# Attention products of the first stage gathered into fewer groups on TensorE, with the last two batches and the hand-over laid out anew

## The chip, the cores and the metric

One of the eight cores of a Trainium2 chip runs the whole program; the seven others are idle. The metric is the device time of one execution in microseconds (us), the median of several runs. A core has TensorE (PE in the profile, with its weight loads as PEld), VectorE (DVE), ScalarE (ACT), GpSimd (POOL) and SyncE (SP, which here issues the DMAs). Each engine works through its own instructions in order, and waits at an instruction for what that instruction needs.

## The reference

Attention with packed queries over eight batches of 576 tokens and eight heads, then two feed-forward layers on all 4,608 tokens.

```python
def sm_attn(qq, kk, vv):
    s = scale * np.matmul(qq, kk.transpose(0, 1, 3, 2))
    s = s - np.max(s, axis=-1, keepdims=True)
    a = np.exp(s)
    a = a / (np.sum(a, axis=-1, keepdims=True) + 1e-09)
    return np.matmul(a, vv)
p_packed = sm_attn(p, k, v)            # 32 packed rows a head
out = sm_attn(q, p_packed, p_packed)   # (8, 8, 576, 64)
...
h = x @ w_in                           # (4608, 512) @ (512, 2048)
x = (h * np.cos(h)) @ w_out            # back to 512
h = x @ w_in2
g = np.where(h >= 1, h, np.where(h <= -1, 0.0, (h + 1) ** 2 / 4))
y = g @ w_out2
```

## The kernel before

The program runs in four stages: the first holds the attention and the first layer up to h; then come h * cos(h) with w_out, w_in2, and w_out2. Only the first stage and its end are touched. All is float32: the large products split each operand into a high and a low part of type fp32r and add three of the four partial products (`TERMS`).

**The first stage** is a list of 128 items, 16 to a batch n. An item (`up`, line 513) is 12 products of 288 columns: it multiplies the second attention's weights `at` of half a batch by a matrix `M` and leaves 256 rows of h for 288 tokens in the PSUM tile `hps` (tag "h", two buffers). ACT copies `hps` into a buffer `u` of SBUF (line 519; four buffers), and SP stores `u` to DRAM as `h1T`; a buffer is free when its store has landed. `M` is the packed values times w_in, one chunk c of 512 columns for four items, in two buffers.

**What else TensorE does in the first stage**, for the batches that come next (`m = n+1` and `m = n+2`), is put between the items by a list of slots: whatever is listed at slot i is issued just ahead of item i. These products are small, and I call them by letters:

- K: `scores1`, packed queries by keys, for half of the 576 tokens (8 products of 288 columns, tile psS).
- T: `turn1`, the transposes of the first attention's weights for one of the two head halves (5 transposes); ACT copies them out as `e` (lines 265 and 266).
- V: `values1`, the weights `e` by the values, for two of the four head pairs (20 products of 32 columns, line 276); ACT copies the sum out as `pt` (line 283).
- Q: `scores2`, queries by packed keys, for half of the tokens (8 products of 288 columns); DVE transposes them out of PSUM (line 294, two instructions a half).
- F: `form`, packed values by w_in for one chunk of `M` (8 products of 512 columns, tile psM); ACT copies the high part out (line 341), DVE the low part (line 343).

K, Q and F use a quarter-by-half tile of the array each, eight at a time. The trace counts every plain float32 product twice. psS and psM are one PSUM tile each, of two banks: whoever writes one waits until it has been read out. `S1` and `S2` are the slots, within a batch, of the steps of the first attention of batch n+2 and of the second of batch n+1; the tuple in the call of `formed` holds those of F. K, T and V, and both halves of Q, go to psS; F goes to psM.

**DVE and ACT** also turn w_out and w_in2 into split form in this stage: `cut_w_out` is a generator of small steps (16 rows f; lines 138 to 157, 391 and 397), of which `WO_SHARE` lets some run behind certain items, and 1.2 us worth behind each item of the last batch. Its loads use two buffers `raw`, so row f+2 is asked for once row f is done.

**The end of the stage.** `begin` issues, ahead of the last six items, the first steps of h * cos(h): `turn_k` to `part_lo` (lines 694 to 721), that make r, the operand of the next stage. That stage sums in PSUM tiles X and Y for even blocks and two tiles Z for odd ones. They take over the banks of "h" and of psS and psM in the order in which they are first asked for: X and Y fall on the two "h" tiles.

A list written in Python sets the order on every engine; no scheduler changes it.

## Time and profile before

| | |
|---|---|
| median of 3 runs | 1497.51 us (1496.89 to 1499.18) |
| the profiled execution, its own time | 1489.83 us |
| its span, first to last instruction | 1488.1 us |
| TensorE busy | 1459.3 us, 98% |
| VectorE, ScalarE busy | 1164.9 us, 908.3 us |
| mean granted clock of TensorE | 0.996 |
| first stage, from the first item to the first product of the next stage | 34.7 to 356.5 us |

TensorE is the busy engine, and from 357 us on it is never idle for long. In the first stage it is busy too, but not all the time, and some of its busy time is spent in changing between small and large products. In a timeline each row gives start, duration, engine, line, operation, out<-in, shape and count of a run of equal instructions, then in brackets how long the engine stood idle before it and what it waited for. Durations of such runs overlap a little at the ends, so the cost of a group is read from its start to the start of the next. A row of waits gives the engine, who waits, for whom, the sum, the number of times and the longest.

### The profile page before, as it was taken

How to read it: one execution, taken by the hardware profiler on the slowest of the kernel's cores; microseconds unless marked ns; L12 is line 12 of the kernel's file. 1: busy time of each engine (PE TensorE's matmuls, PEld its weight loads, DVE VectorE, ACT ScalarE, POOL GpSimd, SP SyncE). 2: the span in 40 equal slices, each digit the busy share in tenths (PEclk: the TensorE clock that was granted, in tenths of full speed). 3: DMA queues.
4: the chain of work that ended last, by engine and by line, in shares of the span. 5: the costliest groups of instructions: out<-in, count | busy, mean ns of one | idle time of the engine just before them, and what ended most of it. 6: DMA issues, size and time to landing. Idle time of an engine off the chain costs nothing.

```text
span 1488.1 us, 29660 instructions
## 1 busy us (share of the span) xinstructions
PE 1459.3 (98%) x11796; PEld 1394.7 (94%) x11796; DVE 1164.9 (78%) x1683; ACT 908.3 (61%) x1424; POOL 134.0 (9%) x85
## 2 busy tenths in 40 slices
PE   8899999998999999999999999999999999999998
PEld 5678777888999999999999999999999999999998
DVE  8885677777898888888856888889868777777875
ACT  4555565657666667666656777877765444444443
POOL 0000000000000000000004435434310000000000
PEclk9999999999999999999999999999999999999999
DMA  9776787477555665866573555654578654344350
GB/s 351 244 245 245 240 285 263 176 264 236 179 159 162 200 186 184 275 217 199 170 273 130 205 181 213 219 180 181 212 290 331 237 160 142 108 130 140 120 160 33
DMA packets 156058, 302.36 MB, mean 203 GB/s; under 512 B 13584, under 2 KB 59664, under 8 KB 152336
## 3 DMA queue, kind: packets, MB, share of 16 engines
q1 hardware_dynamic: 155920, 300.47, 59.7%
q8 instruction: 92, 1.51, 0.4%
q14 instruction: 46, 0.38, 0.1%
HBM read 176.69 MB, written 123.73 MB: 202 GB/s over the span
## 4 chain that ended last, share of the span: by engine, by line
PE 86%; DVE 5%; DMA 5%; ACT 2%; issue 1%; SPq 0%; ACTq 0%; DVEq 0%
PE psZ L748 14%; PE hps L513 10%; PE psZ L955 10%; PE psZ L610 9%; PE psX L748 7%; PE psY L748 7%; PE psX L955 7%; PE psY L955 6%; PE psX L610 6%; PE psY L610 6%; DMA h1T<-u 3%; PE psS L276 1%; PE psM L219 1%; DMA t<-gT 1%; PE psS L219 1%
## 5 line engine op out<-in xcount | busy, mean ns | idle before, releaser
L513 PEld LDWEIGHTS hps<-at,m 128*128 128x128 f32 x1536 | 209.6, 190 | 48.4 <-ACT u L519 18.6
L513 PE MATMUL hps<-at,m 128*128 128x288 f32 x1536 | 227.4, 303 | 10.1 <-ACT at L329 4.7
L748 PE MATMUL psZ<-r,wo 128*128 128x288 f32 x1536 | 206.1, 295 | 0.0
L748 PEld LDWEIGHTS psZ<-r,wo 128*128 128x128 f32 x1536 | 205.2, 188 | 0.0
L858 ACT ACTIVATE r<-g 128x576 fp32r<-128x576 f32 x147 | 97.0, 681 | 122.8 <-DVE g L855 113.7
L77 POOL TENSOR_TENSOR ty<-yb,ty 128x576 fp32r<-128x576 f32 x51 | 86.2, 1691 | 950.3 <-ACT ty L76 949.8
L716 ACT ACTIVATE r<-t 128x576 fp32r<-128x576 f32 x128 | 87.7, 685 | 129.1 <-PE psY L748 62.1
L721 DVE TENSOR_TENSOR r<-t,r 128x576 fp32r<-128x576 f32 x128 | 96.9, 757 | 57.8 <-ACT r L716 57.6
L519 ACT ACTIVATE u<-hps 128x576 f32<-128x576 f32 x128 | 83.1, 650 | 93.7 <-PE hps L513 57.9
L748 PE MATMUL psX<-r,wo 128*128 128x288 f32 x768 | 123.3, 296 | 1.7 <-ACT u L519 1.7
L748 PE MATMUL psY<-r,wo 128*128 128x288 f32 x768 | 123.2, 296 | 0.0
L630 DVE SCALAR_TENSOR_TENSOR t<-hh,t 128x576 f32<-128x576 f32 x128 | 121.8, 971 | 0.0
L622 ACT ACTIVATE t<-hh,half 128x576 f32<-128x576 f32 x128 | 98.9, 772 | 33.2 <-DVE hh L598 31.2
L868 DVE TENSOR_TENSOR r<-g,r 128x576 fp32r<-128x576 f32 x147 | 107.3, 751 | 5.2 <-ACT r L858 5.2
L748 PEld LDWEIGHTS psX<-r,wo 128*128 128x128 f32 x768 | 109.4, 188 | 2.0 <-ACT u L519 2.0
L748 PEld LDWEIGHTS psY<-r,wo 128*128 128x128 f32 x768 | 109.4, 188 | 0.0
L955 PE MATMUL psZ<-r,so 128*128 128x288 f32 x768 | 104.8, 295 | 0.6 <-DVE hh L991 0.6
L955 PE MATMUL psY<-r,sw 128*128 128x288 f32 x768 | 104.6, 295 | 0.0
L955 PEld LDWEIGHTS psZ<-r,so 128*128 128x128 f32 x768 | 102.9, 188 | 0.8 <-DVE hh L991 0.8
L955 PEld LDWEIGHTS psY<-r,sw 128*128 128x128 f32 x768 | 102.8, 188 | 0.0
L711 DVE TENSOR_TENSOR t<-h,t 128x576 f32<-128x576 f32 x128 | 96.1, 751 | 2.2 <-ACT t L706 2.2
L706 ACT ACTIVATE t<-t,halfpi 128x576 f32<-128x576 f32 x128 | 97.6, 762 | 0.0
(163 smaller groups left out, 2642.2 us busy)
## 6 DMA issues: line engine op xcount, KB each, us to landing
h1T<-u SPq DMA_DIRECT2D x128, 288.0 KB, 3.9
h<-h1T SPq DMA_DIRECT2D x128, 288.0 KB, 3.8
gT<-t SPq DMA_DIRECT2D x128, 288.0 KB, 3.2
g<-gT SPq DMA_DIRECT2D x85, 288.0 KB, 3.6
raw<-in_moe_w_out SPq DMA_DIRECT2D x32, 512.0 KB, 6.9
raw<-in_moe_w_in SPq DMA_DIRECT2D x28, 512.0 KB, 6.4
t<-gT SPq DMA_DIRECT2D x36, 288.0 KB, 4.4
k<-in_k SPq DMA_DIRECT2D x8, 1152.0 KB, 9.0
```

The source lines that it names most:

```text
L513: nc.tensor.matmul(out=hps[:, j, :HB], lhsT=m[:, w, G, cs], rhs=x[:, G, y], start=(G == 0 and i == 0), stop=(G == 1 and i == 2),)
L610: nc.tensor.matmul(out=ps[:, i], lhsT=s[:, d, w, cs], rhs=t[:, d, y], start=first and d == n == 0, stop=d == 1 and n == 2, skip_group_chec ...
L622: nc.scalar.activation(out=t, in_=st["h", o], func=AF.Relu, scale=0.5, bias=half)
L630: nc.vector.scalar_tensor_tensor(out=t, in0=st["h", o], scalar=1.0, in1=t, op0=ALU.max, op1=ALU.min)
L706: nc.scalar.activation(out=t, in_=t, func=AF.Sin, scale=2 * PI, bias=halfpi)
L711: nc.vector.tensor_tensor(out=t, in0=G1.pop(i), in1=t, op=ALU.mult)
L716: nc.scalar.activation(out=r[:, 0], in_=turns[i], func=AF.Copy)
L721: nc.vector.tensor_tensor(out=r[:, 1], in0=turns.pop(i), in1=r[:, 0].bitcast(F32), op=ALU.subtract)
L748: nc.tensor.matmul(out=acc[d // 2][:, d % 2], lhsT=wo[f // 4, w][:, f % 4, ds], rhs=r[:, y, k], start=f == n == 0, stop=f == NFT - 1 and n ...
L858: nc.scalar.activation(out=r[:, 0], in_=b[out], func=AF.Copy)
L868: nc.vector.tensor_tensor(out=r[:, 1], in0=src, in1=r[:, 0].bitcast(F32), op=ALU.subtract)
L955: nc.tensor.matmul(out=ps[:, j], lhsT=w_[:, (2 * c + k) % 4, w, j * 128:j * 128 + 128], rhs=r[:, y, k], start=first_k and k == n == 0, sto ...
```

## The change

The slots move so that small products stand together and fewer runs of items lie between them. V becomes one group for all four head pairs, ordered by chunks of 128 tokens, with the heads inside a chunk; only the first chunk's first product clears the sum. The second half of T and the second half of Q go to psM. There are five buffers `u`. F of chunks 1 and 2 stands one item earlier, F of chunk 0 one item later (behind Q), and in the last two batches the low part of the last chunk is cut an item earlier. `WO_LAST` and `WO_MORE` spread the steps of w_out over the last two batches. `begin` starts one item earlier. The two Z tiles of block 1 are asked for first, so they take the banks of "h", and X and Y those of psS and psM.

```diff
+WO_LAST = (1.2, 0, 0, 1.2, 0, 0, 1.2, 1.2, 0, 0, 1.2, 0.6, 0.6, 0.7, 0, 0.7)
+WO_MORE = {3: 0.7, 7: 0.7, 10: 0.7, 11: 0.7}
...
-    def values1(m, G, tag="psS"):
-        if G == 0:
-            PV[m] = double(tag)
-        for hp in (2 * G, 2 * G + 1):
-            for i, (_, n) in enumerate(chunks):
+    def values1(m, tag="psS"):
+        PV[m] = double(tag)
+        for i, (_, n) in enumerate(chunks):
+            for hp in range(HP):
                 for h2 in range(2):
...
-                        rhs=E32[m][:n, h2, i, J * hp:J * hp + J], start=(i == 0), stop=(i == KC),
+                        rhs=E32[m][:n, h2, i, J * hp:J * hp + J], start=(i == hp == 0), stop=(i == KC),
+                        skip_group_check=True,
...
-        u = wk.tile([128, 2, HB], F32, tag="u", name="u", bufs=4)
+        u = wk.tile([128, 2, HB], F32, tag="u", name="u", bufs=5)
...
-                acc = [bank("Z") for _ in range(2)] if blk % 2 else [bank(x) for x in "XY"]
+                acc = early if blk == 1 else [bank("Z") for _ in range(2)] if blk % 2 else [bank(x) for x in "XY"]
...
-        a, b, c, d = scores1(m, 0), scores1(m, 1), turn1(m, 0), turn1(m, 1)
+        a, b, c, d = scores1(m, 0), scores1(m, 1), turn1(m, 0), turn1(m, 1, "psM")
...
-        a, b, c, d, e = scores2(m, 0), scores2(m, 1), soft2(m, 0, 4, V), turn2(m, 0, V), turn2(m, 1, V)
+        a, b, c = scores2(m, 0), scores2(m, 1, "psM"), soft2(m, 0, 4, V)
...
-    S1 = (3, 3, 4, 4, 5, 7, 9, 11, 11, 12, 12, 13, 14, 15)
-    S2 = (1, 1, 2, 2, 3, 4, 5, 7, 8, 9, 10, 10, 11, 12, 13)
+    S1 = (2, 3, 4, 4, 5, 7, 9, 11, 11, 11, 11, 13, 14)
+    S2 = (1, 1, 1, 1, 3, 4, 5, 7, 8, 9, 10, 10, 11, 12, 13)
...
-                formed(j, shifted(base + 4 * c, (1, 1, 2)))
+                formed(j, shifted(base + 4 * c, ((2, 2, 3), (0, 0, 1), (0, 0, 1), (1, 1, 1 if n > B - 3 else 2))[c]))
...
-            if i >= len(items) - 6:
-                for x in begin[i - len(items) + 6]:
+            if i >= len(items) - 7:
+                for x in begin[i - len(items) + 7]:
...
-                t, share = 0.0, 1.2 if i >= 16 * (B - 1) else WO_SHARE.get(i % 16, 0)
+                t, share = 0.0, WO_LAST[i % 16] if i >= 16 * (B - 1) else WO_SHARE.get(i % 16, 0) or (i > 96 and WO_MORE.get(i % 16, 0))
...
+    early = [bank("Z"), bank("Z")]
```

The first place is TensorE early in batch n = 3 (pt_121 are the packed values of batch 4, x12 is one item). Before:

```order
L219 MATMUL psS<-q,pt_121 32x288 x8
L219 MATMUL psM<-wi,pt_124 32x512 x8
L513 MATMUL hps<-at,m 128x288 x12
L219 MATMUL psS<-q,pt_121 32x288 x8
L513 MATMUL hps<-at,m 128x288 x12
L219 MATMUL psS<-k,pp 32x288 x8
L513 MATMUL hps<-at,m 128x288 x12
L219 MATMUL psS<-k,pp 32x288 x8
L513 MATMUL hps<-at,m 128x288 x12
L219 MATMUL psM<-wi,pt_124 32x512 x8
L513 MATMUL hps<-at,m 128x288 x48
```

The same place on TensorE now:

```order
L219 MATMUL psS<-q,pt_121 32x288 x8
L219 MATMUL psM<-q,pt_121 32x288 x8
L513 MATMUL hps<-at,m 128x288 x12
L219 MATMUL psS<-k,pp 32x288 x8
L219 MATMUL psM<-wi,pt_124 32x512 x8
L513 MATMUL hps<-at,m 128x288 x24
L219 MATMUL psS<-k,pp 32x288 x8
L219 MATMUL psM<-wi,pt_124 32x512 x8
L513 MATMUL hps<-at,m 128x288 x48
```

Both Q stand together, in two tiles, and each K stands with an F; the runs of items in front of the long one are two in place of four, and one item lies between the Q in psM and the K and F that need psS and psM again.

The second place is ACT late in the same batch, where it empties T (e) between the copies u of the items and the copy at of the second attention's weights. Before:

```order
L519 ACTIVATE u<-hps 128x576
L265 ACTIVATE e_1757<-psS 128x512
L266 ACTIVATE e_1757<-psS 64x128
L519 ACTIVATE u<-hps 128x576
L329 ACTIVATE at<-a_1755 128x2x288
L265 ACTIVATE e_1757<-psS 128x512
L266 ACTIVATE e_1757<-psS 64x128
L519 ACTIVATE u<-hps 128x576
```

The same place on ACT now:

```order
L519 ACTIVATE u<-hps 128x576
L265 ACTIVATE e_1757<-psS 128x512
L266 ACTIVATE e_1757<-psS 64x128
L265 ACTIVATE e_1757<-psM 128x512
L266 ACTIVATE e_1757<-psM 64x128
L519 ACTIVATE u<-hps 128x576
L329 ACTIVATE at<-a_1755 128x2x288
L519 ACTIVATE u<-hps 128x576
```

The second half of e no longer stands behind a u and an at.

The third place is DVE at the start of batch n = 6, where it empties Q (x<-psS) behind the steps of w_out. Before:

```order
L151 TENSOR_SCALAR raw<-w_3387 128x512
L153 SCALAR_TENSOR_TENSOR raw<-raw 128x512
L397 TENSOR_TENSOR wo<-w_3318,wo 128x512
L294 STREAM_TRANSPOSE x<-psS 128x288 x4
L343 TENSOR_TENSOR m<-psM,m 128x1024
L301 TENSOR_REDUCE mx_3481<-x 128x36
```

The same place on DVE now:

```order
L151 TENSOR_SCALAR raw<-w_3387 128x512
L153 SCALAR_TENSOR_TENSOR raw<-raw 128x512
L397 TENSOR_TENSOR wo<-w_3338,wo 128x512
L294 STREAM_TRANSPOSE x<-psS 128x288 x2
L294 STREAM_TRANSPOSE x<-psM 128x288 x2
L301 TENSOR_REDUCE mx_3480<-x 128x36
L343 TENSOR_TENSOR m<-psM,m 128x1024
```

What stands ahead of the transposes is the same; F's low part (line 343) has moved behind them and behind the first reduction.

## Rows read from the trace of the kernel before

**Rows 1.** The page's first line.
```profile
span 1488.1 us, 29660 instructions
```

**Rows 2.** Timeline of TensorE early in batch 1.
```profile
90.62 0.72 PE L219 MATMUL psS<-kv,pt 64*32 64x288 f32 x16
91.13 1.06 PE L219 MATMUL psM<-wi,pt 64*32 64x512 f32 x16
92.12 1.87 PE L513 MATMUL hps<-at,m 128*128 128x288 f32 x12
93.93 0.71 PE L219 MATMUL psS<-kv,pt 64*32 64x288 f32 x16
94.57 1.86 PE L513 MATMUL hps<-at,m 128*128 128x288 f32 x12
...
102.27 6.66 PE L513 MATMUL hps<-at,m 128*128 128x288 f32 x48
108.86 1.09 PE L219 MATMUL psM<-wi,pt 64*32 64x512 f32 x16
```

**Rows 3.** Timeline of TensorE before the first item: two Q together, then F.
```profile
24.60 1.21 PE L219 MATMUL h<-kv,pt 64*32 64x288 f32 x32 [0.38 <-ACT pt L283]
25.59 1.07 PE L219 MATMUL psM<-wi,pt 64*32 64x512 f32 x16
```

**Rows 4.** Waits of TensorE from 90 to 290 us (batches 1 to 5), all of them.
```profile
PE psS L261 <- ACT e L266: 2.1, 2, 1.8
PE psS L276 <- ACT e L266: 1.9, 2, 1.3
PE psS L219 <- DVE x L294: 1.3, 2, 1.0
PE hps L513 <- ACT u L519: 1.0, 3, 0.5
```

**Rows 5.** Timelines late in batch 2: ACT, then TensorE.
```profile
155.54 0.65 ACT L519 ACTIVATE u<-hps 128x576 f32<-128x576 f32 x1 [2.27 <-DMA h1T<-u]
157.45 1.72 PE L276 MATMUL psS<-e,v 128*64 128x32 f32 x40 [1.28 <-ACT e L266]
```

**Rows 6.** Stretches: length, busy PE, PEld, DVE, ACT, POOL (instructions), granted clock, DMA share, GB/s.
```profile
34.70:90.60 55.90, 49.20 (x512) 39.56 (x512) 48.24 (x85) 31.49 (x57) 0.00 (x0) 0.94 0.74 242
44.60:52.30 7.70, 6.74 (x122) 4.51 (x122) 5.74 (x9) 4.85 (x10) 0.00 (x0) 1.00 0.68 213
158.50:163.50 5.00, 5.00 (x50) 3.10 (x46) 4.90 (x7) 1.03 (x1) 0.00 (x0) 0.66 0.18 62
```

**Rows 7.** Timelines of TensorE and DVE where batches 3, 4 and 6 begin with Q.
```profile
170.11 0.72 PE L219 MATMUL psS<-q,pt 64*32 64x288 f32 x16
173.51 0.84 DVE L294 STREAM_TRANSPOSE x<-psS 128x288 f32<-128x288 f32 x2
...
210.32 0.72 PE L219 MATMUL psS<-q,pt 64*32 64x288 f32 x16
212.98 0.84 DVE L294 STREAM_TRANSPOSE x<-psS 128x288 f32<-128x288 f32 x2
...
289.98 0.71 PE L219 MATMUL psS<-q,pt 64*32 64x288 f32 x16
293.45 0.84 DVE L294 STREAM_TRANSPOSE x<-psS 128x288 f32<-128x288 f32 x2
```

**Rows 8.** Timelines of ACT and TensorE in the last batch and at the hand-over.
```profile
334.88 0.65 ACT L138 ACTIVATE raw<-raw 128x512 f32<-128x512 f32 x1 [3.52 <-DMA raw<-in_moe_w_out]
...
337.04 2.14 PE L513 MATMUL hps<-at,m 128*128 128x288 f32 x14 [2.01 <-ACT u L519]
...
356.50 1.07 PE L748 MATMUL psX<-r,wo 128*128 128x288 f32 x6 [1.72 <-ACT u L519]
```

**Rows 9.** Timeline of TensorE in batch 0, the first T between items.
```profile
76.39 0.76 PE L261 MATMUL psS<-ident,s 128*128 128x128 f32 x5 [0.78 <-DVE s L254]
```

More of the change, by code (lines that the diff above doesn't have):

```diff
@@ L18 @@
 WARM = (10, 14, 10)
-PRI_EXP = 300
 WO_FROM = 36
@@ L27 @@
 WO_SHARE = {0: 1.2, 6: 0.7, 12: 1.3, 13: 1.3, 14: 1.3, 15: 1.3}
-PRI_MAIN = 300
+WO_LAST = (1.2, 0, 0, 1.2, 0, 0, 1.2, 1.2, 0, 0, 1.2, 0.6, 0.6, 0.7, 0, 0.7)
+WO_MORE = {3: 0.7, 7: 0.7, 10: 0.7, 11: 0.7}
 FIRST = ((0, 0), (0, 1), (1, 0), (1, 1), (0, 2), (1, 2), (0, 3), (1, 3))
@@ L1037, in first @@
     def first(m, o):
-        a, b, c, d = scores1(m, 0), scores1(m, 1), turn1(m, 0), turn1(m, 1)
+        a, b, c, d = scores1(m, 0), scores1(m, 1), turn1(m, 0), turn1(m, 1, "psM")
         steps = (nxt(a), nxt(a), nxt(b), nxt(b), lambda: max1(m), lambda: exp1(m), lambda: norm1(m),
-                 nxt(c), nxt(c), nxt(d), nxt(d), lambda: values1(m, 0), lambda: values1(m, 1), lambda: packed(m))
+                 nxt(c), nxt(d), nxt(c), nxt(d), lambda: values1(m), lambda: packed(m))
         for i, (s, x) in enumerate(zip(o, steps)):
@@ L1044, in first @@
                 on(s, lambda: load_k(m + 1))
-            if i == 13 and m + 1 < B:
+            if i == 12 and m + 1 < B:
                 on(s, lambda: load_v(m + 1))
     def second(m, o):
-        a, b, c, d, e = scores2(m, 0), scores2(m, 1), soft2(m, 0, 4, V), turn2(m, 0, V), turn2(m, 1, V)
-        for i, (s, g) in enumerate(zip(o, (a, a, b, b, c, c, c, c, c, d, d, d, e, e, e))):
+        a, b, c = scores2(m, 0), scores2(m, 1, "psM"), soft2(m, 0, 4, V)
+        d, e = turn2(m, 0, V), turn2(m, 1, V)
+        for i, (s, g) in enumerate(zip(o, (a, b, a, b, c, c, c, c, c, d, d, d, e, e, e))):
             on(s, nxt(g))
@@ L1074, in body @@
         if n == 0:
-            first(2, (6, 6, 7, 7, 9, 10, 11, 12, 12, 13, 13, 14, 15, 16))
+            first(2, (6, 6, 7, 7, 9, 10, 11, 12, 12, 12, 12, 14, 15))
         elif n + 2 < B:
@@ L1120, in start @@
         next(a), next(b)
-        values1(0, 0, "h")
-        values1(0, 1)
+        values1(0, "h")
         cut(5)
@@ L1159, in start @@
         cut(5)
-        values1(1, 0)
         next(m1)
-        values1(1, 1)
+        values1(1)
         load_v(2)
@@ L1188, in body @@
              [lambda: turn_s(1), lambda: turn_m(1), lambda: turn_k(3)],
-             [lambda: part_hi(0), lambda: part_lo(0), lambda: turn_s(2), lambda: part_hi(1)]]
+             [lambda: part_hi(0), lambda: part_lo(0), lambda: turn_s(2), lambda: part_hi(1)], []]
     in_order = ordered(E.PE, E.Activation, E.DVE, E.SP, E.Pool)
```

## The prediction

> **What bounds the kernel now.** I read the page first, then the stretches of the first stage, then TensorE's waits there, then its timeline row by row. The span is 1488.1 us [rows 1], and TensorE is the busy engine of all stages. The change touches only the first stage and the hand-over to the second, so the question is what TensorE spends there beyond its products, and which of its waits end on the work that is moved. Three things are to be seen. First, a run of items costs more than its items: one item takes from 92.12 to 93.93, 1.81 us, and four take from 102.27 to 108.86, 6.59 us [rows 2]. So a further item costs (6.59 - 1.81) / 3 = 1.593 us, and each run pays 1.81 - 1.593 = 0.217 us once, for passing to the small products. Second, in batches 1 to 5 TensorE waits 6.3 us in all, 4.0 of them for `e` (T's and V's waits), 1.3 for the transposes of Q, 1.0 for `u` [rows 4]. Third, the last stretch, from Q of batch 6 to the first product of the next stage, takes 356.50 - 289.98 = 66.5 us [rows 7, 8], and it holds waits of its own, 2.01 and 1.72 us being the largest [rows 8]. In the first batch it is DVE that is busy, 48.24 of 55.90 us [rows 6].
>
> **The change part by part.**
>
> **Grouping in batches 1 to 5.** Written in order, a batch on TensorE was QF 1 Q 1 K 1 K 1 F 4 F 2 T 1 T 1 VF 1 V 3 (digits are items), ten runs of items; it becomes QQ 1 KF 2 KF 4 F 3 TT 2 VVF 4, six runs. Four runs fewer save 4 x 0.217; but one of the four lies beside T, which uses the array in the same shape as the items, and I take half for it: 0.76 us. The small groups: Q ahead of F takes 90.62 to 91.13, 0.51; the F behind it 0.99; Q alone 0.64 [rows 2]. K is as large as Q. Before: QF 1.50, Q and two K 1.92, two F 1.98, together 5.40 us (VF and V aside). Two Q together took 0.99 us with F behind them [rows 3], and ahead of an item 0.13 more (0.64 against 0.51): 1.12. After: 1.12, twice KF 3.00, F 0.99, together 5.11. That is 0.29 less. Sum 1.05 a batch, and 5 batches give **5.2 us**. This is work of TensorE itself, so nothing hides it; it is worth less only where a wait takes its place.
>
> **V by chunks of tokens.** The number of products and of weight loads stays, and the two halves of the array alternate as they did. I take 0. The bounds are 0.1 us either way a group, by the 0.13 that a Q differs with its neighbour [rows 2]: 1 us over all batches, both ways. The last chunk's `e` is now needed last, which can only help.
>
> **T's second half in psM, the order of e on ACT, and five buffers u.** In batch 2 ACT stood 2.27 us at a `u` whose buffer was still being stored; the second `e` was queued behind that `u`, and V waited 1.28 us for it [rows 5]. Now the four `e` stand together ahead of that `u`, T's second half needs not wait for psS, two items lie between T and V, and a `u` waits for the store five items back, one item (1.6 us) more. So the 4.0 us for `e` go, and half of the 1.0 for `u` [rows 4]. Behind that wait the clock fell: granted 0.66 from 158.5 to 163.5 [rows 6], so 5.0 x 0.34 = 1.7 us were lost there; I count 1.6 as gone with it. Together 4.0 + 0.5 + 1.6 = 6.1 us.
>
> **Q's second half in psM.** Here a wait is added. DVE reaches the transposes of Q late, because steps of w_out stand ahead of them: 3.40 us behind the start of Q in batch 3, 2.66 in batch 4, 3.47 in batch 6 [rows 7], and what stands ahead of them does not change. A pair takes 0.84, so psS is free at 4.3 and psM at 5.2 us after the start of Q in batch 3 (0.1 for the signal). TensorE comes back to psS with K at 1.12 + 1.81 = 2.9, and to psM with F 0.51 later. K waits 1.4, F then 0.4: 1.8 us. In batch 4: psS 3.6, psM 4.4; waits of 0.6 and 0.3. Batch 5 I take as batch 4; in batches 1 and 2 no steps of w_out stand there yet, and I take none. Sum 1.8 + 0.9 + 0.9 = 3.6 us, in place of 1.3 [rows 4]: **2.3 us lost**. Between 1.3 (DVE is early) and 5 times 1.8 I keep 3.6, from the rows of these very batches. Queued behind the waiting K and F are two items, whose `u` come later by as much; DVE's softmax follows the transposes directly and starts earlier than before, so nothing else is late for it. The Trainium skill has a rule that speaks against this part (TensorEngine Tiling (Array Packing), PSUM Bottleneck): using the array in tiles speeds up the products, not their evacuation, which may become the bound. The rows agree so far as four transposes of 0.42 us stand against 1.12 us of Q; by the rule alone every batch would wait, which is the last rival below.
>
> Batches 1 to 5: 5.2 + 6.1 - 2.3 = **9.0 us**.
>
> **Batches 6 and 7 and the hand-over.** The new order is QQ 1 F 2 F 4 F 5 F 5 F 2 F 4 F 8, 31 items: 31 x 1.593 + 8 x 0.217 = 51.1; QQ 1.12; seven F 6.9: 59.2 us. Added waits: F behind the one item needs psM, free at 3.47 + 1.68 + 0.1 = 5.2, and comes at 2.9: 2.3 us. Of the steps of w_out, one row's load is asked for two items ahead of its use, as all were before; there ACT stood 3.52 us, and TensorE 2.01 [rows 8]. Now one such place is left, and I take half of 2.01: 1.0 us (between 0 and 2.0). Behind the last F, ACT has the copies of eight items, the last two rows of w_out and the first steps of the next stage; I estimate that it is late for the last items by 0.8 us (0 to 2.0, the wait that it caused before). X and Y lie on banks that were read out long before, so the wait of 1.72 us at the hand-over [rows 8] goes, and r is asked for one item earlier, so it isn't late in its place. Sum 59.2 + 2.3 + 1.0 + 0.8 = 63.3 against 66.5: **3.2 us**. What was moved to batch 6 (four shares of w_out, which has no first attention to do) lies on DVE and ACT beside items of TensorE; I cost it at nothing.
>
> **Batch 0.** DVE sets the pace up to the first T, which waited 0.78 us for it [rows 9]; a low part of `M` moves from ahead of one to ahead of another step of the same DVE chain, and I take half of that wait as gone, 0.4. Behind it two runs fewer save 0.4. Together **0.8 us** (0 to 2.5).
>
> **The sum** is 9.0 + 3.2 + 0.8 = 13.0 us off the profiled execution, whose span of 1488.1 becomes 1475.1 and whose own time of 1489.83 becomes 1476.8. The median of the runs lies 7.7 us above that execution; I take the same difference off it: 1497.5 - 13.0 = **1484.5 us**.
>
> **The rivals.**
>
> *The clock falls in the longer stretches of small products.* VVF is now 4.4 us without an item (two V of 1.72 [rows 5], F 0.99 [rows 2]). For it: the clock did fall while V and F ran, 158.5 to 163.5. Against it: from 44.6 to 52.3 there was no item for 7.7 us, only T, V, F and Q with gaps, and the granted clock stayed at 1.00, the 2.4 GHz level [rows 6]. Price: 1.7 us in each of five batches, 8.5: 1493.0. The Trainium skill (TensorE: Matmul & The Clock Gate, Part 1) says that the throttled clock is the default and that recent activity of the array releases it; by that rule fewer gaps help and longer thin stretches may not. Chance 0.08.
>
> *The waits for e and u stay.* If ACT is late for another reason, such as the loads of k that take the queue from the stores, the 6.1 us do not come: 1490.6. For it: a wait of 2.27 is longer than the 1.6 that a buffer buys; against it: `e` no longer stands behind that `u`. Chance 0.12.
>
> *DVE is not late.* The transposes come early, as TensorE itself is what DVE's queue waits for at other places: the 3.6 and 2.3 us do not come: 1478.6. Against it: the steps ahead of them are the same. Chance 0.12.
>
> *psM becomes the bound, and the kernel is slower.* F waits for both pairs of transposes in six batches, 1 to 6: with DVE t us behind the start of Q, the wait is t + 1.78 - 3.44 = t - 1.66. I have 5.9 us in it; 13.0 more, or 3.15 a batch, eat up all gain, so it decides from t = 4.8 in each batch. At t = 6.5 it takes 4.84 x 6 = 29.0, 23.1 more: 1507.6. For it: DVE is the busier of the two that empty PSUM. Against it: t was 3.47 at most. Chance 0.04.
>
> **How the numbers follow.** Forecast 0.64, rivals 0.08, 0.12, 0.12, 0.04. About 0.2%, 3 us, is what a measurement of this kernel tells from no change. The forecast's own bounds (V 1, Q's waits 2.3 less or 5.4 more, w_out and ACT 1.8 less or 2.2 more, batch 0 1.7 less or 0.8 more) hardly fall together; I give it 1479 to 1490. The range goes from 1477 to 1493, which takes in the first three rivals' points, the first at its very edge, and leaves out the last and something of each tail. Faster by over 0.2%: all but the last rival and a small part of the first two, 0.92; within 0.2%: 0.05; slower: 0.03.
>
> **What would show it.** TensorE's groups: Q and K with F in one run, runs of 4, 2, 4, 3, 2 items, 0.217 us a run as before. Its waits from Q of batch 1 to that of batch 6: none for `e`; K and F on psS and psM waiting for line 294 in batches 3 to 6, up to 2.3 us. The granted clock 1.00 from batch 1 on. From Q of batch 6 to the first product on psX some 63 us, with no wait at psX. Wrong would be: new waits of the items for `m` or `at`, a lower clock behind V, or a `u` that still waits 2 us for its store.

## The result, and the profile after

The changed kernel takes 1476.51 us (median of 6 runs, 1473.97 to 1477.79), the kernel before 1497.2 us (6 runs, 1488.2 to 1500.77). The medians lie 20.7 us apart; the ratio on record is 0.9878, with an interval of 0.9855 to 0.9901, which makes 18 us, between 15 and 22. The time lies at the lower end of the predicted range of 1477 to 1493, half a microsecond under it, and 8 us under the predicted 1484.5. The profiled execution of the changed kernel took 1476.36 us, its span is 1474.6 us, where 1475.1 was predicted.

So the span came out and the median did not. And in the span two terms are wrong in opposite directions, as the experiments show. In these rows of the changed kernel (length, busy PE, PEld, DVE, ACT, POOL with instructions, granted clock, DMA share, GB/s) the first two are what lies ahead of batch 1, divided at the Q in batch 0, the third is batches 1 to 5, the fourth batches 6 and 7 up to the first psX product:

```profile
24.00:54.60 30.60, 25.74 (x270) 18.75 (x278) 25.26 (x44) 14.76 (x27) 0.00 (x0) 0.83 0.84 296
54.60:91.10 36.50, 31.39 (x352) 25.77 (x336) 33.62 (x59) 20.79 (x36) 0.00 (x0) 1.00 0.75 243
91.10:279.30 188.20, 183.12 (x2053) 155.26 (x2052) 135.78 (x207) 117.34 (x196) 0.00 (x0) 1.00 0.75 260
279.30:342.00 62.70, 59.77 (x518) 51.66 (x517) 48.43 (x75) 43.19 (x67) 0.00 (x0) 1.00 0.77 258
```

And the same four stretches of the kernel before:

```profile
24.00:51.70 27.70, 23.04 (x262) 17.49 (x263) 24.74 (x44) 15.04 (x28) 0.00 (x0) 0.94 0.92 327
51.70:90.60 38.90, 34.63 (x358) 27.21 (x358) 33.92 (x60) 20.83 (x36) 0.00 (x0) 0.96 0.69 218
90.60:290.00 199.40, 193.04 (x2054) 157.94 (x2054) 135.94 (x207) 117.74 (x196) 0.00 (x0) 0.99 0.72 247
290.00:356.50 66.50, 60.60 (x517) 51.67 (x517) 49.73 (x76) 44.52 (x69) 0.00 (x0) 1.00 0.72 248
```

Batches 1 to 5 lost 11.2 us (9.0 predicted), and 9.9 of them are busy time of TensorE, though the products are the same. Batches 6 and 7 lost 3.8 (3.2 predicted). The part ahead of batch 1 gained nothing in this execution (Q of batch 1 begins at 91.09 us, 90.62 before): the granted clock of its first row was 0.83 against 0.94. Behind the hand-over the execution takes 1.0 us more.

The timeline of TensorE in batch 1 answers [rows 2]; it shows the six runs of items as foreseen, and what was not foreseen, V:

```profile
91.09 0.72 PE L219 MATMUL psS<-kv,pt 64*32 64x288 f32 x16
91.60 0.69 PE L219 MATMUL psM<-kv,pt 64*32 64x288 f32 x16
92.22 1.85 PE L513 MATMUL hps<-at,m 128*128 128x288 f32 x12
94.00 0.71 PE L219 MATMUL psS<-k,pp 64*32 64x288 f32 x16
94.51 1.06 PE L219 MATMUL psM<-wi,pt 64*32 64x512 f32 x16
95.51 3.46 PE L513 MATMUL hps<-at,m 128*128 128x288 f32 x24
...
117.40 2.64 PE L275 MATMUL psS<-e,kv 128*64 128x32 f32 x80
119.98 1.09 PE L219 MATMUL psM<-wi,pt 64*32 64x512 f32 x16
```

Q's pair takes 92.22 - 91.09 = 1.13 us (1.12 predicted), K with F 95.51 - 94.00 = 1.51 (1.50). V, though, takes 119.98 - 117.40 = 2.58 us, where the kernel before had two groups with rows of 1.72 [rows 5], 1.65 from start to start, or 3.30.

TensorE's waits in batches 1 to 5 answer [rows 4]: nothing for `e`, half a microsecond for `u`, and the rest, 4.4 us, is K behind DVE's transposes of Q. (The profile names no releaser for most of it, "issue"; in batch 3 the transposes of psS end at 169.08 us, and K begins at 169.18.)

```profile
PE psS L219 <- issue: 3.8, 2, 2.2
PE psS L219 <- PE hps L513: 0.6, 1, 0.6
PE hps L513 <- ACT u L519: 0.5, 1, 0.5
```

At the end of the stage one wait for `u` is left, and none at psX, where [rows 8] have 2.01 and 1.72 us:

```profile
336.89 5.27 PE L513 MATMUL hps<-at,m 128*128 128x288 f32 x36 [0.74 <-ACT u L519]
342.00 0.97 PE L748 MATMUL psX<-r,wo 128*128 128x288 f32 x6
```

### The profile page after: what moved, and what is told of

The parts are those of the page before. It is cut to its first block, busy times and chain, and to the rows that moved or that the text cites. A ratio compares the mean times of both kernels' runs of the same rounds, so it can differ in the third digit from the quotient of the medians.

```text
span 1474.6 us, 29657 instructions
## 1 busy us (share of the span) xinstructions
PE 1448.3 (98%) x11796; PEld 1391.9 (94%) x11796; DVE 1164.5 (79%) x1683; ACT 908.1 (62%) x1424; POOL 134.1 (9%) x85
## 3 DMA queue, kind: packets, MB, share of 16 engines
q8 instruction: 92, 1.51, 0.4%
## 4 chain that ended last, share of the span: by engine, by line
PE 90%; DVE 4%; DMA 3%; issue 1%; ACT 1%; SPq 0%; DVEq 0%; ACTq 0%
PE psZ L748 14%; PE hps L513 12%; PE psZ L610 10%; PE psZ L955 10%; PE psX L748 7%; PE psY L748 7%; PE psX L955 7%; PE psY L955 6%; PE psY L610 6%; PE psX L610 6%; PE psM L219 2%; PE psS L275 1%; DMA t<-gT 1%; DMA h1T<-u 1%; PE psS L219 1%
## 5 line engine op out<-in xcount | busy, mean ns | idle before, releaser
L513 PE MATMUL hps<-at,m 128*128 128x288 f32 x1536 | 220.9, 301 | 7.7 <-DVE at L331 3.6
L706 ACT ACTIVATE t<-t,halfpi 128x576 f32<-128x576 f32 x128 | 97.6, 763 | 0.0
L699 DVE SCALAR_TENSOR_TENSOR t<-h,t 128x576 f32<-128x576 f32 x128 | 96.2, 751 | 1.7 <-ACT t L694 1.7
```

Source lines behind the costliest of these rows:

```text
L513: nc.tensor.matmul(out=hps[:, j, :HB], lhsT=m[:, w, G, cs], rhs=x[:, G, y], start=(G == 0 and i == 0), stop=(G == 1 and i == 2),)
L699: nc.vector.scalar_tensor_tensor(out=t, in0=G1[i], scalar=1 / (2 * PI), in1=t.bitcast(I32), op0=ALU.mult, op1=ALU.subtract)
L706: nc.scalar.activation(out=t, in_=t, func=AF.Sin, scale=2 * PI, bias=halfpi)
```

## The experiments

They are grouped by the step of the prediction that they test. Each was timed beside the kernel before on the same chip; where two experiments of different sessions are compared, it is by their ratios to the kernel before, which took 1491.6 to 1493.4 us there. "Busy" and "idle" are TensorE's, in batches 1 to 5, from Q of batch 1 to Q of batch 6.

### How much two executions of the same kernel differ

The kernel before and the changed kernel were run once more, without an edit.

> The kernel before itself, profiled and timed once more. The medians of the kernels before and after lie 20.7 us apart, the two profiled executions 13.5 us. Theory (the profiled execution of before, 1489.83, was among its quickest, and the executions of before differ in how long the granted clock falls in the first 350 us): a second profile has the same instructions and waits, with a clock under 0.99 in stretches of batches 1 to 6 that the first profile shows at 0.99 to 1.00, and a span 3 to 10 us longer there. Rival (the difference lies behind 350 us, in the later stages that the change does not touch): batches 0 to 7 end at 356 us again, and the rest takes longer than 1131.6 us.

> The changed kernel itself once more, on the chip and in the minutes of the next three runs, which are held against it. Theory (what scatters from execution to execution is how long the granted clock falls before the first Q of batch 1): its executions spread over 4 us or more, and a second profile gives batches 1 to 5 again 188.2 us within 0.5, with any difference from the first profile in the 91.1 us ahead of them. Rival (the 20.7 us between the first medians are the change's own): the median stays 20 us under that of the kernel before, and the second profile also differs by 7 us more from a second profile of before, in batches 1 to 7.

The kernel before: 1493.59 us (12 runs, 1488.39 to 1498.49), and a second profile of 1495.1 us span. The kernel after: 1476.76 us (6 runs, 1473.48 to 1479.05), ratio 0.9891 (0.9864 to 0.9918), and a second profile of 1471.8 us span. Of the second profile of before, these are the same stretches as above:

```profile
24.00:56.60 32.60, 27.97 (x266) 19.21 (x264) 25.50 (x45) 15.17 (x28) 0.00 (x0) 0.76 0.79 279
56.60:97.60 41.00, 37.56 (x358) 29.29 (x358) 33.51 (x59) 20.84 (x36) 0.00 (x0) 0.86 0.66 204
97.60:294.00 196.40, 191.18 (x2058) 157.27 (x2060) 135.99 (x207) 117.66 (x196) 0.00 (x0) 1.00 0.73 252
```

It reaches Q of batch 1 7.0 us later than the first profile, with a granted clock of 0.76 and 0.86 where that had 0.94 and 0.96. Batches 1 to 5 take 196.4 instead of 199.4, without the clock's fall of [rows 6] (TensorE busy 191.2 for 193.0) and with 1.1 us less waiting. Of the kernel after, batches 1 to 5 take 187.7 us (188.2 the first time), with 183.06 us busy (183.12). So the theory on the kernel before is right that executions differ by their clock, and wrong in the place: it expected the lower clock in batches 1 to 6, and there the second profile was quicker; the lower clock lies ahead of batch 1. The rest behind the hand-over took 4 us more in it; why, is open. For the kernel after the theory holds but for one place: its executions spread over 5.6 us and batches 1 to 5 are the same within 0.5, but batches 6 and 7 differ too, 64.4 us against 62.7, with a fall of the clock in batch 6 (below). What matters for the account: at the same clock of 1.00, batches 1 to 5 differ by 196.4 - 187.7 = 8.7 us, 8.1 of them busy time.

The mean granted clock of each execution is on record for the changed kernel and for all that was timed with the experiments, and it says more than two profiles. Of 57 executions of the kernel before, 28 had a mean clock under 0.994, with a median of 1495.7 us; 16 had 0.997 or more, with a median of 1488.7. Of the changed kernel's 12 executions 1 was under 0.994; the 7 at 0.997 or more have a median of 1475.7. At that clock the two kernels are 13.0 us apart. The rest of what lies between the medians goes with how often the clock fell.

### V by chunks of tokens

```diff
-        for i, (_, n) in enumerate(chunks):
-            for hp in range(HP):
+        for hp in range(HP):
+            for i, (_, n) in enumerate(chunks):
...
-                        rhs=E32[m][:n, h2, i, J * hp:J * hp + J], start=(i == hp == 0), stop=(i == KC),
+                        rhs=E32[m][:n, h2, i, J * hp:J * hp + J], start=(i == 0), stop=(i == KC),
```

> The changed kernel with one thing put back: the 72 products of V run over the heads outside and the token chunks inside again, still in one group. Theory (the order by chunks is itself a gain): V, 2.58 to 2.64 us a group in the changed kernel's trace from batch 2 on, goes back to 3.30 to 3.36 us, the seven V groups cost some 0.7 us more each, all of them on PE's path, so the span grows by 4 to 5 us (1480.5 against 1476). Rival (the order changes nothing, as the prediction has it; what shortened V is the single group): V stays at 2.6 us and the time within 0.5 us.

1485.37 us, ratio 0.9934 (0.9908 to 0.9961): by the ratios 6.4 us slower than the changed kernel when it was run again. (A V has 40 products, and there are eight V; the 72 and the seven of the expectation are slips.) V is back at 3.36 us a row, 2.64 in the changed kernel:

```profile
122.71 3.36 PE L275 MATMUL psS<-e,kv 128*64 128x32 f32 x80
```

Batches 1 and 2, which have no other difference, take 37.22 and 37.10 us against 36.49 and 36.38: **0.73 us for each V**, from the order alone. Among executions with a mean clock of 0.997 or more it takes 1480.6 us (3 of 7) against 1475.7, 5.0 us, where eight V would make 5.8. The other four executions were at 0.991 or 0.992 and took 1485.4 to 1485.9: in the profiled one the clock fell behind a wait in batch 3, and ahead of batch 1 it was 0.76 and 0.90.

The other way round, the kernel before with this part of the change alone:

```diff
-                 nxt(c), nxt(c), nxt(d), nxt(d), lambda: values1(m, 0), lambda: values1(m, 1), lambda: packed(m))
+                 nxt(c), nxt(c), nxt(d), nxt(d), lambda: None, lambda: values1(m), lambda: packed(m))
```

(with `values1` and its calls ahead of the first item as in the changed kernel)

> The kernel before with only the change to V: its 72 products in one group, by token chunks over all heads. Theory (the order is worth 0.72 us a group at full clock, the one group 0.22 us): V 2.6 us where two groups of 1.65 to 1.72 us stood, 0.9 us a batch, 4.7 us in batches 1 to 5, and 6 us in the span: 1482 against a profile of before at the same clock of 1488. Rival (V's order is worth nothing, only the group): 1.1 us in batches 1 to 5, and the wait for e (2.0 us in all ahead of V) changes nothing.

1483.71 us, ratio 0.9940 (0.9920 to 0.9959), 9 us faster than the kernel before. Batches 1 to 5, and TensorE's waits in them:

```profile
89.30:284.20 194.90, 187.75 (x2051) 154.83 (x2050) 135.66 (x207) 116.75 (x196) 0.00 (x0) 1.00 0.73 252
```

```profile
PE psS L219 <- DVE x L294: 2.9, 2, 2.6
PE psS L261 <- ACT e L266: 2.1, 2, 1.7
PE hps L513 <- ACT u L519: 1.8, 3, 0.8
PE psS L219 <- ACT pt L283: 0.2, 1, 0.2
```

Busy time falls by 191.18 - 187.75 = 3.43 us, 0.69 for each V. (My 0.22 for "the one group" does not come: V moved away from F, so the batch still has as many runs of items.) But the stretch is only 196.4 - 194.9 = 1.5 us shorter, since idle time grew from 5.2 to 7.15: Q arrives earlier at a DVE that does not, and waits 2.9 instead of 1.3 [rows 4]; the items wait 1.8 for `u` where the second profile of before has 0.2, and the waits for `e` fall from 3.5 to 2.1. Of the 9 us in the medians these 1.5 and the three V ahead of batch 1, some 2 us, can be placed in the profiles. Part of the rest is how often the clock fell: 1 of these 11 executions had a mean clock under 0.994, and 9 of the 16 of the kernel before that were timed beside them. At 0.997 or more the difference is 6.2 us (1482.5, six executions, against 1488.7).

What makes the order matter? Either a product that adds to the columns just written must wait, or it is something in the order of reading.

```diff
-                        out=PV[m][D * h2:D * h2 + D, 0, J * hp:J * hp + J], lhsT=VR[m][i][:, x:x + D],
+                        out=PV[m][D * h2:D * h2 + D, 0, J * ((hp + i) % HP):J * ((hp + i) % HP) + J], lhsT=VR[m][i][:, x:x + D],
```

(with heads outside, chunks inside, as in the first diff of this part)

> The changed kernel with V's heads outside and chunks inside again, as in the first experiment, so that weights and moving data come in the old order; but each product adds into the columns of the head (head + chunk) mod 4, so that the same 32 columns of PSUM come again only four products later in each half of the array. The sums of the heads are mixed by this and the attention's result is not the reference's; the count and the shapes of the products are unchanged. Theory (what makes the old order slow is that each product adds to the columns that the product before it in its half has just written): V takes 2.6 us a group, as by chunks, and not 3.3 us. Rival (it is the order in which weights or moving data are read): V takes 3.3 us, as in the first experiment.

V stays at 3.36 us in the one execution that was taken, so my theory falls: the columns do not matter.

```profile
122.86 3.36 PE L275 MATMUL psS<-e,kv 128*64 128x32 f32 x80
```

What the old order has and the new has not is seen when V's rows are kept apart by shape. Heads outside (this experiment, the four of batches 1 to 5 whose values lie in `v`; busy us and mean ns behind the bar):

```profile
L275 PE MATMUL psS<-e,v 128*64 128x32 f32 x256 | 10.5, 225 | 0.0
L275 PE MATMUL psS<-e,v 64*64 64x32 f32 x64 | 4.9, 230 | 0.0
```

Chunks outside (the changed kernel):

```profile
L275 PE MATMUL psS<-e,v 128*64 128x32 f32 x256 | 8.2, 223 | 0.0
L275 PE MATMUL psS<-e,v 64*64 64x32 f32 x64 | 2.6, 222 | 0.0
```

The last chunk of tokens has 64 rows instead of 128, and the rows show its products on the array in another shape (64*64 for 128*64). With heads outside that shape is entered and left in each of the four heads, with chunks outside it is entered once. The starts of V's records in the trace say it to the nanosecond: records come in pairs, one pair every 59 ns (steps of 6 or 7 and of 52), and where the shape changes the step of 52 ns becomes one of 149 to 153, about 0.10 us more. In the first experiment a V has seven such steps, in the changed kernel one; six times 0.10, and 0.02 on each neighbouring step, are the 0.72 us (3.14 against 2.42 us from the first start to the last). With the columns rotated the same seven steps are there. The Trainium skill has the rule (TensorEngine Tiling (Array Packing), Key Properties): changing the tiling mode, not just the tile, drains TensorE. The trace fits it, with a pause of 0.10 us at each such change. The prediction had probably priced the same thing without seeing it, as 0.217 us for each run of items, which goes from one shape to another and back; no experiment took that price apart.

### Q, and DVE behind it

```diff
-        a, b, c = scores2(m, 0), scores2(m, 1, "psM"), soft2(m, 0, 4, V)
+        a, b, c = scores2(m, 0), scores2(m, 1), soft2(m, 0, 4, V)
...
-        for i, (s, g) in enumerate(zip(o, (a, b, a, b, c, c, c, c, c, d, d, d, e, e, e))):
+        for i, (s, g) in enumerate(zip(o, (a, a, b, b, c, c, c, c, c, d, d, d, e, e, e))):
...
-    S2 = (1, 1, 1, 1, 3, 4, 5, 7, 8, 9, 10, 10, 11, 12, 13)
+    S2 = (1, 1, 2, 2, 3, 4, 5, 7, 8, 9, 10, 10, 11, 12, 13)
...
-                formed(j, shifted(base + 4 * c, ((2, 2, 3), (0, 0, 1), (0, 0, 1), (1, 1, 1 if n > B - 3 else 2))[c]))
+                formed(j, shifted(base + 4 * c, ((1, 1, 2), (0, 0, 1), (0, 0, 1), (1, 1, 1 if n > B - 3 else 2))[c]))
```

> The changed kernel with the two halves of Q put back into psS, one after the other in slots 1 and 2, and F of the first chunk in slots 1, 1 and 2. Theory (Q together saves one run of items a batch, 0.22 us, over five batches 1.1 us, and costs a second wait at the transposes, 5.3 us in batches 3 to 5 against the 1.3 us of before): undoing it loses the 1.1 us of grouping and gets back up to 4.0 us, so 1473 against 1476, and the PE rows of K behind the DVE transposes, 4.4 us in batches 3 to 5 in the changed kernel, fall to 0.5 us or less. Rival (the lateness of DVE is what counts, not the buffer: the second Q half then waits for psS itself, as before): the waits come back at the second Q, 3 to 5 us, and the time is 1 us longer, 1477.

1480.52 us, ratio 0.9914 (0.9889 to 0.9939), by the ratios some 3 us slower than the changed kernel when it was run again, though the intervals overlap. But the experiment is not a clean one: K stands right behind the second Q now, needs the same buffer, and waits 1.1 us in each of five batches (5.3 us), which the rival had not priced either. So K was put back by a slot as well:

```diff
-    S1 = (2, 3, 4, 4, 5, 7, 9, 11, 11, 11, 11, 13, 14)
+    S1 = (3, 3, 4, 4, 5, 7, 9, 11, 11, 11, 11, 13, 14)
```

> The changed kernel with Q's halves apart in psS again, as in the third experiment, and with the first K put back by one slot as well, so that it does not stand right behind the second Q: the arrangement of Q and K of the kernel before, everything else changed. Theory (Q's gather is worth its runs of items, 0.22 us each, and the wait behind DVE's transposes is there with one buffer or two): the 5.3 us of K waiting behind Q, five times 1.1, that the third experiment had, are gone; batches 1 to 5 take 188 to 190 us against 187.7 to 188.2. Rival (Q together costs more than it saves, as the prediction has it, 3.6 us of waits in place of 1.3): batches 1 to 5 take 186.5 us or less.

1474.57 us, ratio 0.9879 (0.9856 to 0.9902), the same as the changed kernel. Batches 1 to 5 take 189.3 us, and in batch 3 the clock fell, which cost 1.6 us (TensorE busy 38.31 us there, 36.67 in the second profile of the changed kernel): 187.6 without that, against 187.7. In batches 1 and 2, where nothing waits, Q together saves 0.28 and 0.32 us (36.77 and 36.70 against 36.49 and 36.38); in batches 3 to 5 it pays this back in waits. Within what this can tell, Q in two buffers is worth nothing by itself, neither the 1.2 us that the prediction lost on it (1.1 for the run saved, 2.3 for the waits) nor a gain. The wait that all these kernels have has another cause. In the changed kernel, at the start of batch 3 (TensorE, then DVE, then ACT):

```profile
163.96 0.72 PE L219 MATMUL psS<-q,pt 64*32 64x288 f32 x16
...
169.18 0.72 PE L219 MATMUL psS<-k,pp 64*32 64x288 f32 x16 [2.24 <-issue]
...
168.24 0.84 DVE L294 STREAM_TRANSPOSE x<-psS 128x288 f32<-128x288 f32 x2
169.00 0.81 DVE L294 STREAM_TRANSPOSE x<-psM 128x288 f32<-128x288 f32 x2
...
166.48 0.66 ACT L138 ACTIVATE raw<-raw 128x512 f32<-128x512 f32 x1 [1.71 <-DMA raw<-in_moe_w_out]
```

DVE comes to Q 4.28 us after it began: ACT waited 1.71 us for the load of a row of w_out, and DVE's steps on that row stand ahead of the transposes. So the steps were moved to where DVE had idle time:

```diff
-WO_SHARE = {0: 1.2, 6: 0.7, 12: 1.3, 13: 1.3, 14: 1.3, 15: 1.3}
+WO_SHARE = {6: 0.7, 9: 1.2, 11: 1.3, 12: 1.3, 13: 1.3, 14: 1.3}
```

> The changed kernel with one table altered: the steps of w_out's preparation on DVE that stood in slots 15 and 0 of each batch (1.3 and 1.2 us, right ahead of Q's transposes) stand in slots 11 and 9. Theory (what costs after the change is DVE coming late to Q's transposes, because w_out's steps and their load stand ahead of them): the PE waits behind those transposes, 5.3 us in batches 3 to 5 and 2.2 us in batch 6, fall to 1.5 us in all, and the span is 5 to 6 us shorter, 1470 to 1471. Rival (psS is needed at once by K, whatever DVE does, since the transposes themselves take 0.85 us each and ACT and DVE are full in slots 9 and 11): the waits stay at 4 us or more, or come up again in front of at and T, and the time is within 1 us of the changed kernel.

**1467.12 us** (6 runs, 1466.82 to 1472.09), ratio 0.9835 (0.9806 to 0.9865), 9.6 us under the changed kernel of the same session, with no run in common. It is the fastest version found. Start of batch 3, all waits of TensorE in batches 1 to 5, and the two stretches:

```profile
161.41 0.71 PE L219 MATMUL psS<-q,pt 64*32 64x288 f32 x16
...
164.32 0.71 PE L219 MATMUL psS<-k,pp 64*32 64x288 f32 x16
...
163.18 0.84 DVE L294 STREAM_TRANSPOSE x<-psS 128x288 f32<-128x288 f32 x2
```

```profile
PE hps L513 <- DVE m L343: 0.4, 2, 0.2
```

```profile
88.50:271.90 183.40, 182.93 (x2054) 155.41 (x2053) 136.86 (x210) 116.94 (x197) 0.00 (x0) 1.00 0.78 269
271.90:333.00 61.10, 59.89 (x517) 51.68 (x517) 46.65 (x72) 42.75 (x66) 0.00 (x0) 1.00 0.77 257
```

DVE is there 1.77 us after Q, K follows without a wait, and batches 1 to 5 are TensorE's own work but for 0.5 us. The theory holds, the rival falls. In the span the move is worth 1471.8 - 1465.1 = 6.7 us, a little more than expected; the medians differ by 3 us more. That may be the clock: behind the waits that are gone here it sometimes falls, as in the second profile of the changed kernel in batch 6 (TensorE, then the stretch behind it, clock 0.59):

```profile
281.47 1.96 PE L219 MATMUL psM<-wi,pt 64*32 64x512 f32 x16 [2.20 <-DVE x L294]
```

```profile
281.50:285.50 4.00, 4.00 (x27) 2.33 (x28) 2.13 (x2) 1.02 (x1) 0.00 (x0) 0.59 0.03 11
```

In the first profile the same F, behind the same wait of 2.20 us, took 1.09 us, at a clock of 1.00:

```profile
284.47 1.09 PE L219 MATMUL psM<-wi,pt 64*32 64x512 f32 x16 [2.20 <-DVE x L294]
```

In the fourteen profiles TensorE has 18 waits of 2.0 us or more between Q of batch 1 and the first psX; the clock fell behind seven of them. The length does not decide it: it fell behind waits of 2.20, 2.27 and 2.31 us, and stayed at 1.00 behind 2.43, 2.63 and 3.10. The fastest version has no such wait, and four of its six executions have a mean clock of 0.999, a value that one of the changed kernel's twelve reaches.

### The fifth buffer for u

```diff
-        u = wk.tile([128, 2, HB], F32, tag="u", name="u", bufs=5)
+        u = wk.tile([128, 2, HB], F32, tag="u", name="u", bufs=4)
```

> The changed kernel with four buffers for u instead of five. Theory (as the prediction has it, the fifth buffer takes away the waits of ACT's u copy for the store's DMA and the PE waits that follow, and is worth 0.5 to 1.3 us in batches 1 to 5): ACT rows of L519 that wait for a DMA come back, 1 to 3 us of idle time in all, PE waits for u 0.5 to 1.3 us more, the time 1477 against 1476. Rival (ACT has slack there now that the waits for e are gone): 0.0, the same within 0.3 us.

1478.25 us, ratio 0.9909 (0.9874 to 0.9945). ACT's waits for stores are 9.0 us in batches 1 to 5 (1.2 in the changed kernel), but TensorE's waits for `u` are 0.4 us (0.5 there): ACT has room for them. Batches 1 to 5 take 188.95 us against 188.2 and 187.7. The expected 0.5 to 1.3 us of TensorE's waits did not come, so by the waits the rival holds; a difference of about 1 us stays open. With four buffers TensorE has no wait for `e` either, so it is the new place of T and of its copies that took those waits away, and not the fifth buffer.

### Batch 0

```diff
-                formed(j, shifted(base + 4 * c, ((2, 2, 3), (0, 0, 1), (0, 0, 1), (1, 1, 1 if n > B - 3 else 2))[c]))
+                formed(j, shifted(base + 4 * c, ((2, 2, 3), (0, 0, 1), (0, 0, 1) if n else (1, 1, 2), (1, 1, 1 if n > B - 3 else 2))[c]))
```

> The changed kernel with F of the third chunk of batch 0 put back by one slot (steps at 9, 9 and 10 in place of 8, 8 and 9, in batch 0 alone). Theory (the wait of 2.57 us for the low part of at at 73.64 is there because F's low part, 1.22 us, now stands ahead of it on DVE): the PE waits for L331 fall from 3.6 to 1.3 us, and the stretch from the first item to the first Q of batch 1 is 1.5 to 2.5 us shorter at the same clock. Rival (the low part of at is late anyway, behind max1): the wait only moves by 0.5 us, as F stood behind it in the kernel before and the wait for the high part was 2.8 us there.

1477.39 us, ratio 0.9893 (0.9865 to 0.9922): the same. The wait of 2.57 us for the low part of `at` goes, but T then waits 1 us longer. In the first 340 us of this kernel:

```profile
PE psS L261 <- DVE s L254: 1.8, 1, 1.8
PE hps L513 <- DVE at L331: 1.5, 3, 0.6
```

The changed kernel has 0.8 and 3.6 there. Idle time of the stretch from Q in batch 0 to Q of batch 1 (36.90 us with 32.44 busy, against 36.47 with 31.36) falls by 0.65 us, and the clock (0.97 against 1.00) takes it back. The rival was nearer: DVE is busy for 33.6 of 36.5 us here, and its order only chooses who waits.

### The last batches and the hand-over

Both experiments start from the fastest version.

```diff
-                acc = early if blk == 1 else [bank("Z") for _ in range(2)] if blk % 2 else [bank(x) for x in "XY"]
+                acc = [bank("Z") for _ in range(2)] if blk % 2 else [bank(x) for x in "XY"]
...
-            if i >= len(items) - 7:
-                for x in begin[i - len(items) + 7]:
+            if i >= len(items) - 6:
+                for x in begin[i - len(items) + 6]:
...
-    early = [bank("Z"), bank("Z")]
```

> The kernel with w_out's steps in slots 9 and 11 (the sixth experiment) and the hand-over to the next stage put back: the two psZ accumulators are taken where they are used, and the first steps of the next stage begin six items ahead of the end instead of seven. Theory (the hand-over is worth the wait of 1.72 us at the first psX product, and up to 0.8 us of ACT's): the stretch from the first Q of batch 6 to the first psX product takes 62.9 to 63.5 us against 61.2, with a wait at psX of 1.5 us or more. Rival (the wait at psX came from the late work of the last batch, not from the hand-over): no wait at psX, 61.2 us within 0.3, and the time stays 1467.

1471.05 us, ratio 0.9854 (0.9828 to 0.9879). The last stretch takes 63.22 us against 61.17, and the wait at psX is back:

```profile
337.37 1.27 PE L748 MATMUL psX<-r,wo 128*128 128x288 f32 x6 [2.27 <-ACT u L519]
```

The theory holds for the two edits together; they were not tried one by one. Behind that wait the clock was 0.59 for 4 us, which cost 1.6 us more: the first four groups of the next stage take 4.8 us, not 3.2.

```diff
-                t, share = 0.0, WO_LAST[i % 16] if i >= 16 * (B - 1) else WO_SHARE.get(i % 16, 0) or (i > 96 and WO_MORE.get(i % 16, 0))
+                t, share = 0.0, 1.2 if i >= 16 * (B - 1) else WO_SHARE.get(i % 16, 0)
```

> The kernel with w_out's steps in slots 9 and 11 (the sixth experiment) and the old allotment for the last two batches: 1.2 us in each slot of the last batch, no extra steps in the batch before it. Theory (the new tables keep DVE and ACT free in the last eight items, so that ACT's wait of 3.52 us for raw and the PE wait of 2.0 us behind it stay away): with the old ones a PE wait of 1.5 to 2.5 us for u comes back near the end of the last batch, and the stretch from the first Q of batch 6 to the first psX product takes 63 us against 61.2. Rival (with DVE early the old allotment does no harm): 61.2 us within 0.3, and the same time.

1472.2 us, ratio 0.9854 (0.9831 to 0.9878). The stretch takes 63.93 us, 2.8 more, so the size was right, but not the place. It is not an item that waits for ACT's `u`: F waits for the buffer psM, because DVE's low part of the M before it stands behind a row of w_out whose load is late (TensorE, then DVE):

```profile
314.05 1.09 PE L219 MATMUL psM<-wi,pt 64*32 64x512 f32 x16 [3.10 <-DVE m L343]
...
309.92 0.43 DVE L145 TENSOR_SCALAR w<-raw 128x512 int32<-128x512 int32 x1 [2.37 <-ACT raw L138]
```

## Why the prediction was right, and where it was not

| Step | predicted us | measured us | by |
|---|---|---|---|
| Grouping, batches 1 to 5 | -5.2 | -4.7 | busy 183.06 (all) less 187.75 (V alone) |
| V by chunks, batches 1 to 5 | 0 (±1) | -3.4 to -3.7 | busy 187.75 less 191.18; five times 0.73 |
| Waits for e and u | -4.5 | -4.5 | 5.0 before, 0.5 after |
| The clock in batch 2 | -1.6 | -1.9 | busy 191.18 less 193.04 |
| Waits behind Q | +2.3 | +3.9 | 1.3 before; after, 4.4 for K and three times 0.26 for F behind it |
| Batches 6 and 7 | -3.2 | -3.8 | 62.7 less 66.5 |
| Batch 0, from the first item on | -0.8 | +0.4, or -2.1 | first and second profile after, each against the first of before |
| Median over profiled execution | +7.7 | +0.15 | 1476.51 less 1476.36 |

**Right in mechanism and size.** The grouping (six runs, 1.13 and 1.51 us for the small groups; its size in sum is a difference of two kernels, no experiment undid it alone), the waits for `e`, which are gone altogether, the clock in batch 2, F's wait in batch 6 (2.3 predicted, 2.20 measured), the vanished wait at psX. Of ACT's lateness at the end, 0.8 was estimated, and 0.74 stands there, as TensorE's wait for `u`. The wait of 1.0 us for w_out's load in the last batch did not come; batches 6 and 7 are 0.6 better than forecast, so their products cost some 0.5 more. The half microsecond for `u` in batches 1 to 5 came too, but not by the fifth buffer: with four the waits for `u` are 0.4 us.

**V by chunks: the step "the number of products and of weight loads stays; I take 0" failed.** The number stays, the number of shape changes does not: three inside each of the two groups of a V fell to one inside the whole V. A price for going from shape to shape was in the sum already, as 0.217 us a run, and the last chunk's shape (64*64) stands in the rows of V when they are kept apart. This is the largest miss in the span: 3.4 to 3.7 us in five batches, where 1 was the bound. The Trainium skill's sentence on mode switching, given above, would have named it.

**Waits behind Q: the step "what stands ahead of them does not change" failed in part.** In batches 4 and 6 DVE was 2.65 and 3.46 us behind Q, as the prediction took it (2.66 and 3.47). In batch 3 it was 4.28 (taken as 3.40 [rows 7]), with ACT's wait for the load of w_out ahead of it, in a kernel whose TensorE is earlier, and in batch 5 it was 3.62, where I had taken batch 4's 2.66 without a row. Q and its first transposes in batches 4 and 5:

```profile
202.94 0.72 PE L219 MATMUL psS<-q,pt 64*32 64x288 f32 x16
205.59 0.84 DVE L294 STREAM_TRANSPOSE x<-psS 128x288 f32<-128x288 f32 x2
...
241.00 0.71 PE L219 MATMUL psS<-q,pt 64*32 64x288 f32 x16
244.62 0.84 DVE L294 STREAM_TRANSPOSE x<-psS 128x288 f32<-128x288 f32 x2
```

With V alone the same was to be seen: work saved on TensorE ahead of a late DVE partly turns into waiting for it (3.4 us saved, 1.5 kept).

These two errors, -3.5 and +1.6 us, have opposite signs. What they leave of gain in batches 1 to 5, some 2 us, was lost again ahead of batch 1 and behind the hand-over (1.2 and 1.0 us later than forecast). The span was off by 0.5 us only, about what batches 6 and 7 were better. That was luck.

**The median: the step "I take the same difference off it" failed.** The 7.7 us between the profiled execution and the median of the kernel before are not a constant of the measurement. The second profile of before has 7.0 us more ahead of batch 1 at a lower clock, so they go with the clock of an execution. The clocks of the timed executions say it in numbers: at a mean clock of 0.997 or more the kernels are 1488.7 and 1475.7 us, 13.0 apart, and the forecast's sum is 13.0 too, by the same luck; but the kernel before was under 0.994 in 28 of 57 executions, the changed kernel in 1 of 12. The median of the kernel before has the falls of the clock in it, the changed kernel's has not.

That V's order changes how often the clock falls is borne out by the two experiments that change V alone: with V by chunks in the kernel before 1 of 11 executions is under 0.994 (9 of 16 of the kernel before beside it), with heads outside in the changed kernel 4 of 7 (1 of 12 of the changed kernel, timed in other sessions). Where the falls come is seen only in profiles, and less clearly: the four with heads outside reached Q of batch 1 at 90.6, 96.4, 96.6 and 97.6 us, the ten with chunks outside between 88.5 and 93.3. By what V's order does this is not shown.

**The rivals.** The clock did not fall in the VVF stretches (1.00 in both profiles of the changed kernel, batches 1 to 5). The waits for `e` and `u` did not stay. DVE was late, more than forecast, but with 4.28 us at most (4.48 in the second profile) below the 4.8 in every batch from which the kernel would have been slower. The measured time lies closest to the point of the rival "DVE is not late", 1478.6, which did not hold: V and the clock brought it there.

What stays open: why the clock falls behind one wait and not behind another that is as long, the 4 us by which two profiles of the kernel before differ behind the hand-over, and about 1 us for the fifth buffer of `u`.

## What to carry to other kernels

Count the changes of the array's shape, also inside one group of products: a short last chunk in an inner loop changes it twice in each turn of the loop outside, and to put that chunk's products together only the sums of all heads had to stay open at once. When TensorE gets faster, look again at which engine empties its buffers, with its lateness taken against the new start of the product and not the old; here a table of one line that moved DVE's spare work away from that point was worth as much as half the change. And forecast the profiled span and the median separately: look at the granted clock of every timed execution first, since what lies between span and median can be how often it falls, and the change may take that away.

## What the runs showed of the hardware that was not expected

A change between the shapes 128*64 and 64*64 cost 0.10 us (a step of 149 to 153 ns in place of 52), with the same products and the same data; writing to the columns of PSUM that were written just before cost nothing (3.36 us either way). The same wait of 2.20 us in the same kernel was followed once by a granted clock of 0.59 for 4 us and once by 1.00; other falls came behind waits of 2.31 us (Q apart, batch 3) and 2.27 us (at psX), and none behind one of 3.10 us. The order of V's products alone changed how many executions had a mean clock under 0.994: 9 of 16 with heads outside, 1 of 11 with chunks outside.
